# Second batch's attention: scores to ScalarE slot by slot, with the maximum as bias and the sum beside

## The chip, the cores and the metric

One core of a Trainium2 chip runs the whole program as one launch. The time is that of the device, in microseconds, as the median of the runs shown. The profile is of one more execution, which has a time of its own.

The engines of the core are named as the profile names them: PE is TensorE (PEld its weight loads), DVE is VectorE, ACT is ScalarE, POOL is GpSimd, SP issues most DMAs. Each engine takes its instructions strictly in the order in which the program wrote them, and waits for the other engines by semaphores.

## The reference

Three stages in a row, all in float32.

- Attention over 2 batches, 8 heads, 576 positions, head size 64. Heads 0 to 3 see the 32 latest positions (local); heads 4 to 7 see earlier positions with the same remainder modulo 32 (strided):

```python
scores = scale * q @ k.T                      # scale = 1/8
scores = where(mask, scores, -1e9)
scores = scores - max(scores, -1)
attn = exp(scores)
attn = attn / (sum(attn, -1) + 1e-9)
x = attn @ v                                  # then 1152 tokens x 512
```

- A gated product: `a = x @ w1; b = x @ w2; h = (a * b) @ w3; x = h @ w_out`.
- Four experts, mixed by given probabilities: `out += p_e * (relu(x @ w1_e) @ w2_e)`.

## The kernel before

Every large product is made of three matmuls on a high and a low part of both operands (`mm3`, L264 to L268, which is why L266, L267 and L268 carry nearly all the matmuls of the profile). ScalarE rounds to the high part, VectorE subtracts for the low one.

**Attention** is cut into chunks (`Chunk4`): per batch three local ones (c = 0, 1, 2 of g = 0) and three strided ones (g = 1), so six, numbered 0 to 5 below. A local chunk holds 6 slots of 64 score columns in one PSUM bank, a strided one 8 slots of 54. Each of the 128 partitions is one query row of its slot. A chunk goes through `scores` (PE), `maxima` (L367: VectorE takes the maximum of each slot and writes scores minus maximum to a frame `p_ring` in SBUF), `exps` (L380: one ScalarE activation over the whole frame, with the scale 1/8), `sums` (L383: VectorE sums each slot, adds 1e-9, takes the reciprocal), `normalise` (L394: VectorE in the second batch, GpSimd in the first), `transposes` (PE, into a PSUM bank), `evac` (L403: ScalarE copies it to SBUF), `pv` (PE, into two banks), `put` (ScalarE, high part of the result) and `put_lo` (VectorE, low part).

**Order.** All of it is in an order written out by hand (`tc.manual_schedule`, L748). The first batch's chunks run alone at the start (L816 to L848). The second batch's six chunks are woven into the first batch's gated product: `run_unit` (L772) emits one unit of that product, two accumulations of 12 matmuls each; ScalarE copies the first accumulation out (L503), VectorE multiplies it with the second (L505). After units 2, 4, 5, 7, 8, 10, 11, 13 and 14 comes one call of `attend` (L787). Call s emits, in this order: the scores of chunk s+1, `maxima` and `exps` of chunk s, `sums` and `normalise` of chunk s-1, `pv`, `put` and `put_lo` of chunk s-3, `transposes` and `evac` of chunk s-2. Below, "step s" is what follows the maximum of chunk s, until that of chunk s+1.

Each unit also calls a worker twice (`advance`, L256) which turns the next weights from 64-bit to 32-bit floats: ScalarE rounds (L143) and takes the magnitude (L151), VectorE clamps (L154), shifts (L157), adds the sign (L160) and the low bits (L164); then ScalarE makes the high part (L172) and VectorE the low one (L182). A unit can't start before the weights it uses are ready.

**Buffers.** Products, transposes and `pv` share five PSUM banks (`ps`); scores have three of their own (`ps_sc`). A bank that a transpose filled comes free when `evac` is through, one that a product filled when L503 or L505 is.

GpSimd in the second batch only does one small memset per strided chunk (L374, for the 1e-9 in the sum).

Of the kernel before, what the change touches and what calls it, by code (L numbers as in the profile page):

```python
# [8 lines left out]
F32 = mybir.dt.float32  # L9
# [4 lines left out]
AF = mybir.ActivationFunctionType  # L14
# [4 lines left out]
P = 128  # L19
# [13 lines left out]
SCALE = 1.0 / float(D) ** 0.5  # L33
# [9 lines left out]
def kernel(  # L43
# [13 lines left out]
    nc = tc.nc  # L57
# [8 lines left out]
    small = ctx.enter_context(tc.tile_pool(name="small", bufs=4))  # L66
# [254 lines left out]
    class Chunk4:  # L321
# [45 lines left out]
        def maxima(self):  # L367
            s = self.slots
            mx = small.tile([P, 8], F32, tag="mx", name="mx")
            nc.vector.tensor_reduce(out=mx[:, :s], in_=self.sc, axis=mybir.AxisListType.X, op=ALU.max)  # L370
            self.frame = p_ring[self.index % 4]
            self.p = self.frame[:, :s, :self.nk]
            if self.g:
                nc.gpsimd.memset(self.frame[:, :, T3:T3 + 1], 1e-9)  # L374
            nc.vector.tensor_tensor(out=self.p, in0=self.sc, in1=self.wide(mx), op=ALU.subtract)
# [2 lines left out]
            return t[:, :self.slots].unsqueeze(2).to_broadcast([P, self.slots, self.nk])  # L378

        def exps(self):  # L380
            nc.scalar.activation(self.p, self.p, AF.Exp, scale=SCALE)

        def sums(self):  # L383
            s = self.slots
            self.rec = small.tile([P, 8], F32, tag="rec", name="rec")
            rec = self.rec[:, :s]
            if self.g:
                nc.vector.tensor_reduce(out=rec, in_=self.frame[:, :s, :T3 + 1], axis=mybir.AxisListType.X, op=ALU.add)
            else:
                nc.vector.tensor_reduce(out=rec, in_=self.p, axis=mybir.AxisListType.X, op=ALU.add)  # L390
                nc.vector.tensor_scalar_add(rec, rec, 1e-9)
            nc.vector.reciprocal(rec, rec)
# [188 lines left out]
    class Weights:  # L581
# [17 lines left out]
        def work(self):  # L599
# [20 lines left out]
            if self.again:  # L620
                for i, u in enumerate(sums):
                    nc.sync.dma_start(out=u.bitcast(F32), in_=stored[self.at][i])
            else:
                yield from self.split(sums, w)
                for i, u in enumerate(sums):
                    nc.sync.dma_start(out=stored[self.at][i], in_=u.bitcast(F32))
# [394 lines left out]
```

## Time and profile before

| | |
|---|---|
| runs shown | 626.92, 626.93, 627.87 us; median 626.93 us |
| the profiled execution | 628.45 us, its span 626.3 us |
| PE busy | 615.6 us, 98% of the span |
| VectorE busy | 450.4 us, 72% |
| ScalarE busy | 265.0 us, 42% |
| GpSimd busy | 10.1 us, 2% |
| mean granted clock of PE | 0.997 of full |
| second batch's chunks, first maximum to last `put_lo` | 42.7 to 96.7 us |

A row of a timeline gives start, duration, engine, line, operation, what is written and read, and in brackets the idle time of that engine before it, with the instruction that ended it. Merged instructions carry their count (x2). Durations overlap at the ends: on ScalarE the next instruction starts about 0.1 us before the end of the one before it, if it has nothing to wait for. A busy PE is a PE with matmuls under way, not one at its peak.

### The profile page before, as it was taken

The numbers are of one execution on the slowest core, as the hardware profiler recorded it, in microseconds if no ns is written. First come the engines' busy times: TensorE is split into PE (matmuls) and PEld (weight loads), VectorE is DVE, ScalarE is ACT, GpSimd is POOL, SyncE is SP. The second block draws the span as 40 slices with busy tenths as digits, with TensorE's granted clock in tenths as the row PEclk, the third lists the DMA queues.
The fourth block names the chain that finished last, engine by engine and source line by source line (L and its number), as shares of the span: only waits on it lengthen the run. The fifth ranks groups of instructions, "written<-read, shape, count | busy, mean of one in ns | idle before, by whom it ended". The sixth has DMA issues, their size and how long they took to land.

```text
span 626.3 us, 11330 instructions
## 1 busy us (share of the span) xinstructions
PE 615.6 (98%) x4632; PEld 559.5 (89%) x4632; DVE 450.4 (72%) x813; ACT 265.0 (42%) x455; POOL 10.1 (2%) x37
## 2 busy tenths in 40 slices
PE   8899999999999999999999999999999999999997
PEld 5598899999889999999989999899889898989996
DVE  4889995989784224867977888788775665755843
ACT  3564574765654123433343433434433333333320
POOL 4100000000000000000000000000000000000000
PEclk9899999999999999999999999999999999999999
DMA  8876330235522210344344344354586566565411
GB/s 262 291 272 190 127 137 2 92 124 186 205 78 97 95 68 1 135 163 174 135 166 170 136 173 163 135 188 159 196 297 253 181 224 219 186 214 189 154 49 67
DMA packets 28726, 99.43 MB, mean 159 GB/s; under 512 B 2652, under 2 KB 6740, under 8 KB 26116
## 3 DMA queue, kind: packets, MB, share of 16 engines
q1 hardware_dynamic: 28132, 98.14, 44.5%
q8 instruction: 36, 0.59, 0.4%
q10 hardware_dynamic: 544, 0.59, 0.3%
q14 instruction: 14, 0.11, 0.1%
HBM read 79.58 MB, written 19.14 MB: 158 GB/s over the span
## 4 chain that ended last, share of the span: by engine, by line
PE 88%; DVE 4%; DMA 3%; ACT 3%; issue 2%; POOL 0%; SPq 0%; DVEq 0%
PE g_acc L266 11%; PE g_acc L267 11%; PE g_acc L268 10%; PE m_a L268 4%; PE m_a L267 4%; PE m_a L266 4%; PE m_b L267 3%; PE m_c L266 3%; PE x_acc L268 3%; PE x_acc L267 3%; PE x_acc L266 3%; PE m_c L267 3%; PE m_b L266 3%; PE m_c L268 3%; PE m_b L268 3%; PE ab_acc L266 3%
## 5 line engine op out<-in xcount | busy, mean ns | idle before, releaser
L657 ACT ACTIVATE h_hi<-u 128x320 fp32r<-128x320 f32 (+1 forms) x128 | 56.9, 445 | 189.0 <-DVE u L663 189.0
L266 PE MATMUL g_acc<-w_hi,h_hi 128*128 128x512 f32 (+1 forms) x296 | 114.3, 386 | 0.0
L267 PE MATMUL g_acc<-w_lo,h_hi 128*128 128x512 f32 (+1 forms) x296 | 114.2, 386 | 0.0
L268 PE MATMUL g_acc<-w_hi,h_lo 128*128 128x512 f32 (+1 forms) x296 | 113.7, 384 | 0.0
L596 DVE TENSOR_TENSOR w_lo<-raw,w_hi 128x768 fp32r<-128x768 f32 x64 | 69.4, 1084 | 12.4 <-ACT w_hi L594 12.4
L663 DVE TENSOR_TENSOR u<-m_b,u 128x320 f32<-128x320 f32 (+1 forms) x96 | 40.7, 452 | 51.1 <-PE m_b L268 51.1
L266 PE MATMUL ab_acc<-x_hi,w_hi 128*128 128x288 f32 x252 | 75.2, 298 | 1.3 <-ACT pT L406 1.0
L268 PE MATMUL ab_acc<-x_hi,w_lo 128*128 128x288 f32 x252 | 74.2, 294 | 0.0
L267 PE MATMUL ab_acc<-x_lo,w_hi 128*128 128x288 f32 x252 | 74.2, 294 | 0.0
L268 PEld LDWEIGHTS g_acc<-w_hi,h_lo 128*128 128x128 f32 x296 | 55.6, 188 | 11.6
L266 PEld LDWEIGHTS g_acc<-w_hi,h_hi 128*128 128x128 f32 x296 | 55.8, 188 | 8.0
L267 PEld LDWEIGHTS g_acc<-w_lo,h_hi 128*128 128x128 f32 x296 | 55.7, 188 | 7.6
L659 DVE SCALAR_TENSOR_TENSOR h_lo<-u,h_hi 128x320 fp32r<-128x320 f32 (+1 forms) x128 | 57.6, 450 | 3.6 <-ACT h_hi L657 1.8
L594 ACT CAST w_hi<-raw 128x768 fp32r<-128x768 f32 x64 | 59.9, 936 | 0.0
L266 PEld LDWEIGHTS ab_acc<-x_hi,w_hi 128*128 128x128 f32 x252 | 47.3, 188 | 2.0 <-ACT pT L406 1.2
L267 PEld LDWEIGHTS ab_acc<-x_lo,w_hi 128*128 128x128 f32 x252 | 47.3, 188 | 0.0
L268 PEld LDWEIGHTS ab_acc<-x_hi,w_lo 128*128 128x128 f32 x252 | 47.3, 188 | 0.0
L267 PE MATMUL m_b<-b_t,s_hi 128*128 128x320 f32 (+1 forms) x128 | 37.9, 296 | 0.0
L663 DVE TENSOR_TENSOR u<-m_a,u 128x320 f32<-128x320 f32 (+1 forms) x64 | 28.9, 451 | 11.6 <-PE m_a L268 11.6
L596 DVE TENSOR_TENSOR s_lo<-raw,s_hi 128x1024 fp32r<-128x1024 f32 x16 | 19.6, 1225 | 24.3 <-ACT s_hi L594 24.3
L663 DVE TENSOR_TENSOR u<-m_c,u 128x320 f32<-128x320 f32 (+1 forms) x64 | 29.0, 452 | 4.5 <-PE m_c L268 3.9
L673 ACT COPY u<-m_a 128x320 f32<-128x320 f32 (+1 forms) x32 | 12.7, 398 | 42.3 <-PE m_a L268 42.3
(162 smaller groups left out, 1398.2 us busy)
## 6 DMA issues: line engine op xcount, KB each, us to landing
raw<-in_e_dram SPq DMA_DIRECT2D x32, 1024.0 KB, 5.1
raw<-in_w_dram SPq DMA_DIRECT2D x8, 1024.0 KB, 6.4
raw<-in_w3T_dram SPq DMA_DIRECT2D x8, 1024.0 KB, 4.9
stored<-s_hi SPq DMA_DIRECT2D x16, 512.0 KB, 2.6
stored<-s_lo SPq DMA_DIRECT2D x16, 512.0 KB, 2.6
s_hi<-stored SPq DMA_DIRECT2D x16, 512.0 KB, 3.5
s_lo<-stored SPq DMA_DIRECT2D x16, 512.0 KB, 6.9
raw<-in_w_out_dram SPq DMA_DIRECT2D x4, 1024.0 KB, 8.4
```

What stands on the lines that cost most here:

```text
L266: mm(acc, lh, rh, start=first, stop=False)
L267: mm(acc, lh, rl, start=False, stop=False)
L268: mm(acc, ll, rh, start=False, stop=last)
L594: nc.scalar.copy(dst[0], src)
L596: nc.vector.tensor_tensor(out=dst[1], in0=src, in1=dst[0].bitcast(F32), op=ALU.subtract)
L657: nc.scalar.activation(hi, src, AF.Relu)
L659: nc.vector.scalar_tensor_tensor(out=lo, in0=src, scalar=0.0, in1=hi.bitcast(F32), op0=ALU.max, op1=ALU.subtract)
L663: nc.vector.tensor_tensor(out=out, in0=acc, in1=b, op=ALU.add)
L673: nc.scalar.copy(u1, a)
```

## The change

For the second batch (`self.b` is 1) alone:

- `maxima`: VectorE still takes the maximum of each slot. It no longer subtracts; GpSimd multiplies the maxima by -1/8 in place.
- `exps`: in place of one activation over the frame in SBUF, ScalarE runs one per slot (6 or 8). Each reads its scores from PSUM, takes the slot's scaled maximum as a bias column, and gives the slot's sum beside its result.
- `sums`: no summing on VectorE; GpSimd adds 1e-9 to the sums, VectorE takes the reciprocal as before.
- The memset of the 1e-9 column is gone for the second batch.

```diff
@@ maxima
             self.p = self.frame[:, :s, :self.nk]
+            if self.b:
+                self.mx = mx
+                nc.gpsimd.tensor_scalar_mul(mx[:, :s], mx[:, :s], -SCALE)
+                return
             if self.g:
                 nc.gpsimd.memset(self.frame[:, :, T3:T3 + 1], 1e-9)
             nc.vector.tensor_tensor(out=self.p, in0=self.sc, in1=self.wide(mx), op=ALU.subtract)
@@ exps
+            if self.b:
+                self.rec = small.tile([P, 8], F32, tag="rec", name="rec")
+                for s in range(self.slots):
+                    at = slice(s, s + 1)
+                    nc.scalar.activation(self.p[:, s], self.sc[:, s], AF.Exp, bias=self.mx[:, at], scale=SCALE,
+                                         accum_out=self.rec[:, at])
+                return
             nc.scalar.activation(self.p, self.p, AF.Exp, scale=SCALE)
@@ sums
             s = self.slots
-            self.rec = small.tile([P, 8], F32, tag="rec", name="rec")
+            if not self.b:
+                self.rec = small.tile([P, 8], F32, tag="rec", name="rec")
             rec = self.rec[:, :s]
-            if self.g:
+            if self.b:
+                nc.gpsimd.tensor_scalar_add(rec, rec, 1e-9)
+            elif self.g:
```

## Rows read from the trace of the kernel before

**Rows 1.** Waits of PE from 30 us on: total, times, longest.

```profile
PE ab_acc L266 <- ACT pT L406: 1.0, 1, 1.0
PE tp L401 <- DVE p_ring L396: 0.9, 1, 0.9
...
PE ab_acc L266 <- ACT ab L503: 0.3, 1, 0.3
```

**Rows 2.** Windows: stretch, length, busy time of each engine, PE clock, DMA, GB/s.

```profile
70.00:80.00 10.00, 9.02 (x109) 8.46 (x107) 9.79 (x18) 5.93 (x12) 0.00 (x0) 1.00 0.08 16
```

**Rows 3.** Timeline of VectorE, 42 to 78 us: start, duration, what.

```profile
42.73 0.55 DVE L370 TENSOR_REDUCE mx<-sc 128x6 f32<-128x384 f32 x1
...
44.75 0.46 DVE L505 TENSOR_TENSOR ab_f<-ab_acc,ab 128x288 f32<-128x288 f32 x1 [0.28 <-ACT ab L503]
...
50.20 0.55 DVE L370 TENSOR_REDUCE mx<-sc 128x6 f32<-128x384 f32 x1
...
53.71 1.21 DVE L182 TENSOR_TENSOR w_lo<-t,w_hi 128x1024 fp32r<-128x1024 f32 x1
...
55.45 0.55 DVE L370 TENSOR_REDUCE mx<-sc 128x6 f32<-128x384 f32 x1
...
60.62 0.68 DVE L154 TENSOR_SCALAR t<-t 128x1024 f32<-128x1024 f32 x1
...
63.56 0.60 DVE L370 TENSOR_REDUCE mx<-sc 128x8 f32<-128x432 f32 x1
...
66.21 0.61 DVE L458 TENSOR_TENSOR x_lo<-o,x_hi 128x192 fp32r<-128x192 f32 x2
...
69.37 0.60 DVE L370 TENSOR_REDUCE mx<-sc 128x8 f32<-128x432 f32 x1
...
71.93 0.61 DVE L458 TENSOR_TENSOR x_lo<-o,x_hi 128x192 fp32r<-128x192 f32 x2
...
77.92 0.60 DVE L370 TENSOR_REDUCE mx<-sc 128x8 f32<-128x432 f32 x1
```

**Rows 4.** Timeline of ScalarE, 43 to 81 us.

```profile
43.91 0.53 ACT L381 ACTIVATE p_ring<-p_ring 128x384 f32<-128x384 f32 x1 [3.25 <-DVE p_ring L375]
44.34 0.38 ACT L503 COPY ab<-ab_acc 128x288 f32<-128x288 f32 x1
44.62 1.05 ACT L172 CAST w_hi<-t 128x1024 fp32r<-128x1024 f32 x1
...
57.05 0.46 ACT L406 COPY pT<-tp 128x384 f32<-128x384 f32 x1
...
58.76 1.16 ACT L151 ACTIVATE t<-raw 128x1024 f32<-128x1024 f32 x1
...
79.67 0.52 ACT L454 CAST x_hi<-o 128x192 fp32r<-128x192 f32 x2
80.08 0.60 ACT L406 COPY pT<-tp 128x512 f32<-128x512 f32 x1
```

**Rows 5.** Timeline of PE: the `pv` of the second batch's chunk 3.

```profile
80.73 0.83 PE L427 MATMUL o<-pT,tv_str 54*64 54x54 f32 x32 [0.62 <-ACT pT L406]
```

**Rows 6.** Groups of ScalarE by shape: count, busy us, mean ns, idle before.

```profile
L381 ACT ACTIVATE p_ring<-p_ring 128x432 f32<-128x432 f32 x6 | 3.4, 566 | 12.7 <-DVE p_ring L375 12.7
...
L381 ACT ACTIVATE p_ring<-p_ring 128x384 f32<-128x384 f32 x6 | 3.1, 524 | 17.7 <-DVE p_ring L375 17.7
...
L111 ACT ACTIVATE one<-idle 128x1 f32<-128x1 f32 x1 | 0.2, 202 | 0.0
```

**Rows 7.** Timeline of all engines, 25.2 to 27 us, first batch's last chunk.

```profile
25.27 0.20 DVE L392 RECIPROCAL rec<-rec 128x8 f32<-128x8 f32 x1
...
25.61 0.92 POOL L396 TENSOR_TENSOR p_ring<-p_ring,rec 128x432 f32<-128x432 f32 x1 [2.90 <-DVE rec L392]
...
26.50 0.12 POOL L374 MEMSET p_ring<- 128x8 f32 x1
```

**Rows 8.** A window in the first batch, PE clock last but two.

```profile
17.00:23.00 6.00, 4.80 (x89) 3.64 (x85) 4.49 (x11) 2.94 (x8) 1.94 (x5) 0.72 0.85 320
```

## The prediction

> **What bounds the kernel now.** I read the waits of PE first. The page's first part has PE busy 98% of the span, so a change can only move the end by making PE wait more or less. From 30 us on PE waits for little: 1.0 us for ScalarE's copy of a transpose, 0.9 us for VectorE's normalised frame, 0.6 us for another such copy, 0.3 us later for L503 [rows 1, 5]. The first three lie in the second batch's attention, the stretch that the change touches. They are all that it could give back there: 0.6 + 0.9 + 1.0 = 2.5 us.
>
> Next the windows. In that stretch VectorE has hardly any idle time, 9.79 of 10 us from 70 to 80, ScalarE 5.93, GpSimd none [rows 2]. PE has run ahead and waits for the others. So VectorE's queue sets the pace there, and ScalarE stands idle 3.25 us in front of an exp until VectorE has subtracted [rows 4].
>
> Last the timelines of VectorE and ScalarE, to see what each does between one maximum and the next, and which of the two the other then waits for. The idle time of ScalarE is no free room: what stands behind the exp in its queue (the copies L503 and L406, the casts L454, the weights' L172 and L151) is what VectorE and PE wait for next.
>
> **What goes.** VectorE loses six subtractions, six sums and three additions of 1e-9, some 1.2 us a chunk, and gets a wait in their place: the reciprocal of chunk s-1 stands right behind the maximum of chunk s, and now needs GpSimd's addition, which stands in GpSimd's queue behind the multiplication for chunk s. POOL loses three memsets that nobody waited long for; I cost them at nothing. ScalarE loses six activations over a whole frame.
>
> **What comes, per slot.** 3 x 6 + 3 x 8 = 42 activations of 64 or 54 columns with a sum. No row shows one. Two bounds. From 384 to 432 columns an exp goes from 524 to 566 ns, 0.875 ns a column [rows 6]; carried down to 64 columns that is 524 - 320 x 0.875 = 244 ns. The next instruction on ScalarE starts 0.10 us before the end (43.91 + 0.53 to 44.34) [rows 4], so a bare one takes 0.145 us of the queue: the lower end, with bias column and sum for nothing. At the upper end the sum is an instruction of its own, as long as the shortest activation shown, 202 ns [rows 6], and nothing overlaps: 0.244 + 0.202 = 0.45 us. I take the sum as such an instruction that does overlap, 0.20 - 0.10 = 0.10, and for the bias column, which must be fetched too, 0.07 of the same 0.10: 0.145 + 0.10 + 0.07 = 0.32 us a slot. 1.92 us for a local chunk, 2.56 us for a strided one, where one activation took 0.43 us of the queue.
>
> The Trainium skill ("ScalarE: Activation LUTs", section "What ACT_TABLE_LOAD costs") prices an activation with a bias column at 280 ns plus 0.833 ns a column, less 93 ns overlap; without one at 186 ns. Its price without the column gives 506 ns for 384 columns, and the trace has 524, so they nearly agree. By it, with my 0.10 for the sum, a slot would cost 0.34 us (0.33 for 54 columns), and the sum below would be 7.5 us in place of 6.9. It speaks against this change: each slot pays the fixed part anew.
>
> **GpSimd.** From VectorE's end to a waiting GpSimd is 25.27 + 0.20 to 25.61, 0.14 us [rows 7]. Its multiplication of 6 or 8 columns lies between a memset of 8 columns, 0.12, and a product of 432, 0.92 [rows 7]; I take 0.20, near the memset. From there 0.04 us to ScalarE (as VectorE's maximum and subtraction to the exp). So the first slot starts 0.38 us behind the end of a maximum; the exp started 0.63 us behind it (42.73 + 0.55 to 43.91) [rows 3, 4].
>
> The Trainium skill ("SBUF — State Buffer", section "Who interferes with whom") says that a GpSimd instruction is held up while VectorE runs a one-input instruction in its two-port mode. Only chunk 0 has one there, the clamp that follows the maximum at once (later chunks have the waiting reciprocal). By that rule the first multiplication would start about 0.5 us later and the sum be 7.4 us; no row shows such a meeting, and I leave it out.
>
> **The sum, step by step.** Each step is measured from the end of a maximum to the first instruction that the later ScalarE holds up; the difference shifts all that follows on VectorE, the next maximum too. Slots end at 0.38 + 1.92 = 2.30 us behind the maximum in local chunks, at 0.38 + 2.56 = 2.94 in strided ones.
>
> - Step 0: the copy L503 stands behind the exp, 0.38 us long, and VectorE's product waits for it. After: 2.30 + 0.38 + 0.03 = 2.71. Before: 43.28 to 44.75, 1.47 [rows 3, 4]. Late by 1.24 us.
> - Step 1: L503, then 0.28 us later L172, 1.05 us long, and VectorE's L182 waits for it. After: 2.30 + 0.28 + 1.05 + 0.03 = 3.66. Before: 50.75 to 53.71, 2.96 [rows 3, 4]. Late by 0.70 us.
> - Step 2: `evac`, L503, L143 and the magnitude L151; from the first to the last 58.76 - 57.05 = 1.71, then 1.16. VectorE's clamp waits. After: 2.30 + 1.71 + 1.16 + 0.03 = 5.20. Before: 56.00 to 60.62, 4.62 [rows 3, 4]. Late by 0.58 us.
> - Step 3: the casts of `put` stand behind the exp; two start 0.205 us apart and end after 0.52, so the first takes 0.31 [rows 4]. `put_lo` waits for it. After: 2.94 + 0.31 + 0.04 = 3.29. Before: 64.16 to 66.21, 2.05 [rows 3]. Late by 1.24 us.
> - Step 4: the same. Before: 69.97 to 71.93, 1.96 [rows 3]. Late by 1.33 us.
> - Step 5: PE's `pv` of chunk 3 waits for `put` (0.41) and `evac` (0.60). After: 2.94 + 0.41 + 0.60 + 0.04 = 3.99. Before: 78.52 to 80.73, 2.21 [rows 3 to 5]. Late by 1.78 us.
>
> Sum: 1.24 + 0.70 + 0.58 + 1.24 + 1.33 + 1.78 = 6.87 us. PE waited for this very `pv` before, and afterwards waits for nothing but the 0.3 us of a later load [rows 1], so the lateness stays: no slack behind it takes it back. VectorE's saved work lies in front of these waits and turns into idle time there. PE's own waits at the transposes grow along the way but are no further term, since PE catches up only to the same copies.
>
> As a formula: 42 slots x their cost - 6.57 us. Zero at 0.156 us a slot; -0.5 us at the lower bound 0.145, +12.3 us at 0.45. GpSimd's share is six multiplications: a memset's 0.12 us each would take off 0.5 us, a product's 0.92 would add 4.3.
>
> Against the profiled execution's own 628.45 us this makes 635.3. That one stands 1.5 us above the median of the runs shown, 626.93; on the median the forecast is 633.8 us.
>
> **Rivals.**
>
> *PE's clock falls.* In six microseconds of the first batch in which PE was idle for 1.2 the granted clock was 0.72 on the mean, so part of them ran at the lower level, 1.2 GHz, and (1 - 0.72) x 6 = 1.7 us of PE were lost [rows 8]. In the changed kernel PE would wait about 0.62 + 1.78 = 2.4 us at `pv` of chunk 3, and as long in the two steps before. A drop in those is swallowed by the next wait; one behind the last isn't: 633.8 + 1.7 = 635.5. Against it: around these waits PE has dense products, which it hadn't in the first batch.
>
> *Slots at the upper bound.* Each sum is read only when its activation is through. For it: the sum does need the last column. +12.3 us, 639.3.
>
> *Slots as cheap as bare ones.* ScalarE then isn't late, and VectorE, 0.7 us a chunk better off, releases the frames and copies sooner; PE's three waits shrink. For it: VectorE is the engine without idle time [rows 2]. It decides below 0.156 us a slot. At 0.12 us the formula gives -1.5: 625.4; the waits of PE allow 624.4 at best. Against it: 0.12 is under the line through the exps.
>
> *It changes nothing that can be measured*: slots between 0.126 and 0.186, where gain and lateness cancel; 627.
>
> **How the numbers follow.** About 0.2% is what a measurement of this kernel can tell from no change, 1.25 us. Chances: forecast 0.65 (slots 0.20 to 0.43), clock 0.15, upper bound 0.10, no change 0.05, faster 0.05. So slower 0.90, same 0.05, faster 0.05. The range leaves out the last three, 0.20: low 629.0 is a slot of 0.20 (+1.8), high 638.5 one of 0.43 (+11.5) or a dearer slot than mine with a clock drop on top.
>
> **What would show it.** ScalarE has 42 short exps in six bursts, each 1.9 to 2.6 us; the time from one slot to the next is the number that decides. VectorE idles 1 to 2 us before L503's product in step 0 and before `put_lo` in steps 3 to 5, put down to ScalarE, and about 0.5 us before each reciprocal, put down to GpSimd. PE waits over 2 us three times for a copy of a transpose, and not later. After 95 us the two timelines run alike, some 7 us apart. The forecast is wrong if a slot costs under 0.19 us, if PE's waits don't grow, or if PE's clock row falls below 1.00 after 85 us.

## The result, and the profile after

The changed kernel takes 636.01 us, median of four runs (635.25 to 637.28); the kernel before, run beside it, 627.4. The ratio is 1.0135, 95% interval 1.0116 to 1.0154: slower, as forecast. The time is 2.2 us above the 633.8 of the prediction. The profiled execution took 635.94 us, with a span of 634.2 us against 626.3.

PE's waits from 30 us on in the changed kernel (what waited, for what; total us, times, longest), to be read against [rows 1]:

```profile
PE o L432 <- ACT pT L420: 2.4, 1, 2.4
PE o L441 <- ACT pT L420: 2.3, 1, 2.3
PE ab_acc L266 <- ACT ab L517: 1.2, 2, 0.8
PE tp L415 <- DVE p_ring L410: 1.0, 1, 1.0
PE ab_acc L266 <- DVE x_lo L472: 0.6, 1, 0.6
PE ab_acc L268 <- DVE w_lo L182: 0.4, 1, 0.4
PE ab_acc L512 <- ACT w_hi L172: 0.4, 1, 0.4
```

Two waits of over 2 us stand at `pv`, both for ScalarE's copy of a transpose (timeline of PE, chunks 1 and 3):

```profile
70.04 0.90 PE L432 MATMUL o<-pT,tv_loc 64*64 64x32 f32 x48 [2.40 <-ACT pT L420]
...
87.04 0.79 PE L441 MATMUL o<-pT,tv_str 54*64 54x54 f32 x32 [2.32 <-ACT pT L420]
```

The later one has grown from 0.62 [rows 5]; the earlier one is new, and the 1.0 at the product behind it has become 0.6. The wait for VectorE's normalised frame is what it was. VectorE's own part got shorter, and PE gained nothing from it.

ScalarE in the changed kernel, chunk 0 of the second batch (start, duration), to be read against the one exp in [rows 4]:

```profile
43.80 0.31 ACT L389 ACTIVATE p_ring<-sc,mx 128x64 f32<-128x64 f32 x1 [3.37 <-POOL mx L375]
44.01 0.19 ACT L389 ACTIVATION_READ_ACCUMULATOR p_ring<-sc,mx 128x1 f32 x1
44.10 0.30 ACT L389 ACTIVATE p_ring<-sc,mx 128x64 f32<-128x64 f32 x1
...
45.25 0.33 ACT L389 ACTIVATE p_ring<-sc,mx 128x64 f32<-128x64 f32 x1
45.45 0.23 ACT L389 ACTIVATION_READ_ACCUMULATOR p_ring<-sc,mx 128x1 f32 x1
45.54 0.42 ACT L517 COPY ab<-ab_acc 128x288 f32<-128x288 f32 x1
```

A slot is two instructions: an activation, and a readout of the accumulated sum that starts 0.20 us later; 0.09 us after that the next slot starts. From 43.80 to 45.54 are 1.74 us for six slots, 0.29 each. The copy L517, for which VectorE waits, stands behind all of them. The same instructions by shape (count, busy us, mean ns, idle before):

```profile
L389 ACT ACTIVATION_READ_ACCUMULATOR p_ring<-sc,mx 128x1 f32 x42 | 9.0, 213 | 0.0
L389 ACT ACTIVATE p_ring<-sc,mx 128x54 f32<-128x54 f32 x24 | 6.9, 316 | 6.4 <-POOL mx L375 6.4
L389 ACT ACTIVATE p_ring<-sc,mx 128x64 f32<-128x64 f32 x18 | 5.4, 318 | 9.0 <-POOL mx L375 9.0
```

Against [rows 6]: a slot of 54 columns is busy for 316 ns, a whole frame of 432 was for 566.

VectorE, in steps 0, 3 and 5 of the changed kernel, to be read against [rows 3]:

```profile
42.50 0.55 DVE L370 TENSOR_REDUCE mx<-sc 128x6 f32<-128x384 f32 x1
42.97 0.68 DVE L154 TENSOR_SCALAR t<-t 128x1024 f32<-128x1024 f32 x1
46.00 0.46 DVE L519 TENSOR_TENSOR ab_f<-ab_acc,ab 128x288 f32<-128x288 f32 x1 [2.35 <-ACT ab L517]
...
65.81 0.60 DVE L370 TENSOR_REDUCE mx<-sc 128x8 f32<-128x432 f32 x1
67.09 0.19 DVE L406 RECIPROCAL rec<-rec 128x6 f32<-128x6 f32 x1 [0.69 <-POOL rec L400]
...
69.42 0.62 DVE L472 TENSOR_TENSOR x_lo<-o,x_hi 128x192 fp32r<-128x192 f32 x2 [1.54 <-ACT x_hi L468]
...
86.31 0.62 DVE L472 TENSOR_TENSOR x_lo<-o,x_hi 128x192 fp32r<-128x192 f32 x2 [1.47 <-ACT x_hi L468]
```

In brackets is what became of the work that VectorE was spared: 2.35 us of waiting before the product of step 0, 0.7 to 0.8 before the reciprocals (all but the last), 1.4 to 1.5 before each `put_lo` of steps 3 to 5. From the end of the maximum to the held instruction step 0 now takes 46.00 - 43.05 = 2.95 us, where it took 1.47.

Last, windows of the changed kernel (stretch, length, busy time of PE, PEld, DVE, ACT, POOL; the granted clock is the last number but two), to be read against [rows 2]:

```profile
70.00:80.00 10.00, 9.38 (x99) 9.02 (x99) 7.42 (x14) 8.28 (x26) 0.51 (x2) 0.83 0.01 2
71.00:72.00 1.00, 1.00 (x8) 1.00 (x9) 1.00 (x3) 1.00 (x2) 0.00 (x0) 0.82 0.09 16
72.00:73.00 1.00, 1.00 (x6) 1.00 (x5) 1.00 (x2) 0.46 (x1) 0.00 (x0) 0.50 0.00 0
...
88.00:94.00 6.00, 6.00 (x36) 6.00 (x35) 5.50 (x11) 4.03 (x9) 0.00 (x0) 0.72 0.01 3
```

Between 70 and 80 us VectorE went from 9.79 us busy to 7.42 and ScalarE from 5.93 to 8.28: the pace has changed hands. (The two stretches don't hold quite the same work, since the changed kernel runs some 3 us behind there.) And PE's clock is at its lower level, 1.2 GHz (0.50), from about 71.6 to 75 us and again from about 88.7 to 92, each time 1.6 us after the end of one of the two long waits, with matmuls in between. The first fall loses (1 - 0.83) x 10 = 1.7 us of PE, the second (1 - 0.72) x 6 = 1.7. In the kernel before, the windows from 30 us on have the clock at 1.00.

### The profile page after: what moved, and what is told of

It reads as the page before. It is cut to its first block, busy times and chain, and to the rows that moved or that the text cites. A ratio compares the mean times of both kernels' runs of the same rounds, so it can differ in the third digit from the quotient of the medians.

```text
span 634.2 us, 11401 instructions
## 1 busy us (share of the span) xinstructions
PE 619.6 (98%) x4632; PEld 562.3 (89%) x4632; DVE 444.3 (70%) x798; ACT 274.6 (43%) x533; POOL 13.1 (2%) x46
## 4 chain that ended last, share of the span: by engine, by line
PE 83%; issue 5%; ACT 4%; DVE 3%; DMA 3%; POOL 0%; POOLq 0%; SPq 0%; DVEq 0%
PE g_acc L266 10%; PE g_acc L267 10%; PE g_acc L268 10%; PE m_a L268 4%; PE m_a L267 4%; PE m_a L266 4%; PE m_b L267 3%; PE m_c L266 3%; PE x_acc L268 3%; PE x_acc L267 3%; PE x_acc L266 3%; PE m_c L267 3%; PE m_b L266 3%; PE m_c L268 3%; PE m_b L268 3%
## 5 line engine op out<-in xcount | busy, mean ns | idle before, releaser
L266 PE MATMUL ab_acc<-x_hi,w_hi 128*128 128x288 f32 x252 | 76.7, 304 | 1.8 <-ACT ab L517 1.2
L268 PE MATMUL ab_acc<-x_hi,w_lo 128*128 128x288 f32 x252 | 75.7, 300 | 0.4 <-DVE w_lo L182 0.4
L267 PE MATMUL ab_acc<-x_lo,w_hi 128*128 128x288 f32 x252 | 75.7, 300 | 0.0
L266 PEld LDWEIGHTS ab_acc<-x_hi,w_hi 128*128 128x128 f32 x252 | 48.6, 193 | 2.7 <-ACT ab L517 1.7
L268 PEld LDWEIGHTS ab_acc<-x_hi,w_lo 128*128 128x128 f32 x252 | 48.7, 193 | 0.7 <-DVE w_lo L182 0.7
L267 PEld LDWEIGHTS ab_acc<-x_lo,w_hi 128*128 128x128 f32 x252 | 48.7, 193 | 0.0
```

The lines of the kernel that those rows point to most:

```text
L266: mm(acc, lh, rh, start=first, stop=False)
L267: mm(acc, lh, rl, start=False, stop=False)
L268: mm(acc, ll, rh, start=False, stop=last)
```

## The experiments

Theory A: the number of activations and readouts on ScalarE makes it late for the copies behind them in its queue, and PE's clock adds to it. The rivals put the cost on GpSimd's round trips, on the move of work as such, or on the clock alone. Ratios are against the kernel before, run beside each.

**e1: the small work on VectorE.** The multiplication and the addition leave GpSimd.

```diff
-                nc.gpsimd.tensor_scalar_mul(mx[:, :s], mx[:, :s], -SCALE)
+                nc.vector.tensor_scalar_mul(mx[:, :s], mx[:, :s], -SCALE)
-                nc.gpsimd.tensor_scalar_add(rec, rec, 1e-9)
+                nc.vector.tensor_scalar_add(rec, rec, 1e-9)
```

> The changed kernel, its small operations (times -1/8, plus 1e-9) on VectorE in place of GpSimd. Theory A (ScalarE's longer bursts make VectorE and PE late by some 6.3 us, and PE's clock falls once behind the last wait for 1.7 us): only the start of each burst moves. With GpSimd it starts 0.36 to 0.75 us behind a maximum; a small VectorE operation of 0.17 us and 0.03 us before it make that 0.24 us, so six times 0.13 and 0.4 in step 0: about 1.2 us less than the changed kernel, 634.8 us. Rival B (the two ways to GpSimd and back in each chunk are the cost: 0.38 us before the exps, 0.7 us before the reciprocal): some 6 us less, 630 or below.

632.87 us, ratio 1.0091 (1.0066 to 1.0115): between the two. PE's waits at `pv` were as long as before the edit, 2.3 and 2.1 us, so GpSimd didn't make them. But in the profiled execution the clock didn't fall behind them (its mean is 1.000):

```profile
70.00:76.00 6.00, 4.08 (x31) 3.85 (x30) 4.12 (x10) 4.97 (x22) 0.00 (x0) 1.00 0.00 0
88.00:94.00 6.00, 6.00 (x75) 5.78 (x74) 5.79 (x14) 4.16 (x6) 0.00 (x0) 1.00 0.10 15
```

So the 3 us under the changed kernel could be GpSimd's or the clock's; e17 takes that up.

**e2: the sums on VectorE.** No accumulating output; VectorE sums and adds as before the change, and GpSimd's memset of the 1e-9 column is back.

```diff
-                    nc.scalar.activation(self.p[:, s], self.sc[:, s], AF.Exp, bias=self.mx[:, at], scale=SCALE,
-                                         accum_out=self.rec[:, at])
+                    nc.scalar.activation(self.p[:, s], self.sc[:, s], AF.Exp, bias=self.mx[:, at], scale=SCALE)
...
-            if self.b:
-                nc.gpsimd.tensor_scalar_add(rec, rec, 1e-9)
-            elif self.g:
+            if self.g:
```

> The changed kernel without the sum beside the exp: VectorE sums each chunk again and adds the 1e-9 as in the kernel before; bias, slots and GpSimd's multiplication stay. The trace of the changed kernel has 0.095 us of ScalarE's queue for each reading of a sum. Theory A: 42 x 0.095 = 4.0 us less, since VectorE's sums fall into time in which it waited for ScalarE; 632.0 us, and 630.3 if PE's clock then doesn't fall. Rival B (GpSimd's round trips): one of two goes, about 3 us less, but then the time before each reciprocal shrinks and not the bursts. Rival D (VectorE's relief was worth something and is given back): slower than A says by the six sums, 3.4 us, so 635.5.

630.3 us, ratio 1.0051 (1.0035 to 1.0068): A, at its value for a clock that holds, though in the profiled execution the clock fell once, from 83 to 86 us. The timeline of its ScalarE, a local chunk and a strided one (the bare slots are merged, x6 and x8):

```profile
42.81 1.34 ACT L390 ACTIVATE p_ring<-sc,mx 128x64 f32<-128x64 f32 x6 [3.35 <-POOL mx L377]
44.01 0.43 ACT L515 COPY ab<-ab_acc 128x288 f32<-128x288 f32 x1
...
70.25 1.68 ACT L390 ACTIVATE p_ring<-sc,mx 128x54 f32<-128x54 f32 x8 [1.16 <-POOL p_ring L375]
71.77 0.59 ACT L466 CAST x_hi<-o 128x192 fp32r<-128x192 f32 x2
```

To the next instruction are 1.20 and 1.52 us: 0.20 and 0.19 a slot. The readout is the other 0.09. Six readouts less are 0.5 us a chunk that stood ahead of a held copy.

**e3: the split alone.** The kernel before, its exp cut into slots in SBUF; no bias column, no sum, VectorE and GpSimd untouched.

```diff
+            if self.b:
+                for s in range(self.slots):
+                    nc.scalar.activation(self.p[:, s], self.p[:, s], AF.Exp, scale=SCALE)
+                return
             nc.scalar.activation(self.p, self.p, AF.Exp, scale=SCALE)
```

> The kernel before with one edit: the second batch's exp of a frame is split into one activation per slot (42 in place of 6), from SBUF, without bias column and without sum; VectorE and GpSimd as before. A (the number of activations on ScalarE makes ScalarE late): a slot without the sum took 0.19 to 0.20 us of ScalarE's queue in the changed kernel; in the formula 42 x 0.195 - 6.57 = 1.6, plus the exp's start 0.63 in place of 0.38 us behind the maximum, 6 x 0.25 = 1.5: 3.1 at most, less where VectorE's own subtractions and sums still stand in front of the held instruction; 627.3 + 1 to 3.1 = 628.3 to 630.4. F (splitting alone costs nothing, the sums and GpSimd's part cost it all): 627.3 +- 0.5.

629.44 us, ratio 1.0030 (1.0017 to 1.0042): A, in the middle of its range. Its ScalarE:

```profile
43.54 1.00 ACT L383 ACTIVATE p_ring<-p_ring 128x64 f32<-128x64 f32 x6 [3.25 <-DVE p_ring L375]
44.44 0.38 ACT L507 COPY ab<-ab_acc 128x288 f32<-128x288 f32 x1
...
64.95 1.22 ACT L383 ACTIVATE p_ring<-p_ring 128x54 f32<-128x54 f32 x8 [3.05 <-DVE p_ring L375]
66.08 0.51 ACT L458 CAST x_hi<-o 128x192 fp32r<-128x192 f32 x2
```

0.90 us for six and 1.13 for eight: 0.15 and 0.14 us for a bare slot, the lower bound of the prediction. Even so 2 us are lost.

**e6: the changed kernel, with the exps out of the way.** They are issued behind the step's copies and casts and behind the next unit's first copy.

```diff
@@ attend
-                chunk[s].exps()
...
+            if s < n:
+                later.append(chunk[s].exps)
@@ run_unit, behind the first half of the next unit
+                for exps in later:
+                    exps()
+                later.clear()
```

> The changed kernel with each burst of exps emitted later in ScalarE's queue: behind put, evac and the next unit's first copy, with nothing else changed. Theory A: what VectorE and PE waited for now stands ahead of the burst, steps 0 and 3 to 5 lose their lateness, steps 1 and 2 (weights' casts behind the burst) keep some; PE no longer waits over 2 us, its clock stays up. Near the kernel before, 627 to 629 us. Rival B (GpSimd's round trips, which stay, all of them): no better than the changed kernel less 2 us, 634 or more.

626.5 us, ratio 0.9994 (0.9982 to 1.0006): A, half a microsecond under its range. Every instruction of the change is still there; only what stands behind the slots is another.

**e7: the same move in the kernel before.** It settles whether e6 undid a lateness or gained something else that hid it.

```diff
-                chunk[s].exps()
+            if s < n:
+                later.append(chunk[s].exps)
```

> The kernel before with one edit: the second batch's exp of a frame is issued on ScalarE behind the copies of the step and the next unit's first copy, as in e6, with one activation per frame and all of VectorE's work as before. A (in e6 the move only took the slots out of the way of the held instructions; the exp of before was 0.43 us of the queue, so the move has little to give): 626.3 to 627.3. G (the move itself gains several us, and the changed instructions cost as much in e6 as in the changed kernel, hidden by that gain): below 624, since e6 was 9.5 us faster than the changed kernel.

627.0 us, ratio 0.9991 (0.9975 to 1.0006): A. Over all executions the move alone is worth nothing that can be measured, and 1.3 us where the mean clock is 0.999 or more (medians 625.7 for six executions, 627.0 for 14 of the kernel before); in the changed kernel it was worth 9.5 us (636.0 to 626.5). So the place of the slots in ScalarE's queue is the cause, the clock included, as far as the queue brings it about.

**e10: the clock held up.** The changed kernel, with eight idle matmuls of 448 columns ahead of `pv` in steps 4 and 6.

```diff
                 c = chunk[s - 3]
+                if s in (4, 6):
+                    acc = ps_sc.tile([P, 512], F32, tag="sc", name="warm")
+                    for _ in range(8):
+                        mm(acc[:, :448], flat(i_loc), flat(m_loc), start=True, stop=True)
                 c.pv()
```

> The changed kernel with eight idle matmuls of 448 columns on PE ahead of pv in steps 4 and 6, that is inside the two waits of 2.3 to 2.4 us, into a bank of the scores. Theory A: the clock no longer falls behind either; the first fall was swallowed by the next wait, the second is worth 1.7 us, so 634.3 us; VectorE's and ScalarE's times up to pv of chunk 3 stay. Rival C (the clock is most of the loss, PE's waits would be hidden without it): 630 or below. Rival E (the clock costs nothing, it is the same lateness counted twice): 636, unchanged.

632.5 us, ratio 1.0080 (1.0053 to 1.0106), and the same two windows now read:

```profile
70.00:76.00 6.00, 5.65 (x82) 4.66 (x79) 4.28 (x8) 4.78 (x19) 0.51 (x2) 1.00 0.04 12
...
88.00:94.00 6.00, 6.00 (x52) 5.96 (x47) 5.60 (x12) 4.74 (x10) 0.00 (x0) 1.00 0.01 3
```

PE does more work and the kernel is 3.5 us faster by the medians. The idle matmuls also shorten the idle stretches: PE stands for 1.60 us ahead of the first eight, which wait for the exps to free a bank of scores, and for 0.78 us ahead of the later `pv`. The time is under the 634.3 that A expected, with the first fall swallowed by the next wait and the second worth 1.7; why, is said with the prediction below.

**e17: e1 with e10's idle matmuls.** Both edits are shown above.

> e1 (the two small instructions on VectorE) with the idle matmuls of e10 ahead of pv in steps 4 and 6, so that PE's clock is the same in both. K (with the clock held, it is all the same whether GpSimd or VectorE does the small work: e1 was 3.1 us under the changed kernel because the clock cost it less): as e10, 631.5 to 633.2, ratio 1.007 to 1.009. L (GpSimd's way there and back costs the 3 us itself): 629 to 630.3, ratio 1.003 to 1.005.

632.81 us, ratio 1.0087 (1.0063 to 1.0112), beside e10's 1.0080: K by the medians, and L's 3 us are excluded. A smaller price shows in the traces. From the start of the first maximum to `pv` of chunk 3 are 43.4 us in e1 and in e17, 44.6 in e10 and 44.5 in the changed kernel: GpSimd's way costs some 1.2 us up to there, as A had it in e1, and the medians don't resolve it. That e1 itself was no slower (1.0091), though its three other executions had a mean clock of 0.995, says that falls cost it little; why they did, and why its clock held in the profiled one, behind waits as long as those of the changed kernel, stays open.

**e18: e2 with idle matmuls.** Here they came to stand behind `pv` and `put`, not ahead of them as in e10, which the expectation did not reckon with.

> e2 (no accumulating output, sums on VectorE) with the idle matmuls of e10. A (42 readouts of 0.09 us of ScalarE's queue are the dearest part, with the clock held too): e10 less 3.8 us, 628.0 to 629.3, ratio 1.001 to 1.003. M (the readouts cost little, and e2 was faster because its clock fell once and not twice): 630.5 to 632.5, ratio 1.005 or more.

632.34 us, ratio 1.0077 (1.0056 to 1.0098). It does not decide between A and M: behind `pv` the 16 idle matmuls are on PE's path, and in one window the clock fell all the same:

```profile
82.00:88.00 6.00, 5.15 (x50) 3.57 (x51) 5.44 (x12) 3.46 (x10) 0.00 (x0) 0.72 0.18 74
```

The wait, 1.93 us, comes first, and the work after it didn't keep the clock up here. What the sums cost at full clock is seen otherwise: the executions of e2 with a mean clock of 0.999 or more took 629.6, 630.0 and 630.25 us, those of e10 632.1, 632.3 and 632.7. The sums on ScalarE, with GpSimd's addition, are worth some 2.3 us at the end; A had said 3.8. Up to `pv` of chunk 3 the traces are nearer to A: from the start of the first maximum 41.0 us in e2, 44.6 in e10.

**e13: what is good in the change.** e6 with e2's sums: the subtraction stays gone, the slots stand out of the way, and the reciprocal waits for nothing on GpSimd.

> The changed kernel with two edits: exps behind the copies as in e6, and the sums back on VectorE (no accumulating output; the sum and the addition of 1e-9 as the kernel before has them), so that the reciprocal waits for nothing on GpSimd; the slots still read PSUM with the scaled maximum as bias, and VectorE has no subtraction. A (what stays of the change is then VectorE's saved subtractions, and the slots are out of the way): the six waits of 0.69 to 0.82 us for GpSimd in e6 go, six sums of about 0.4 us come back: 626.5 - 6 x (0.75 - 0.4) = 624.4, range 623.5 to 626. H (GpSimd's round trip costs nothing in e6, VectorE only waits there instead of later): 626.5 + up to 2.4 = 627 to 629.

Its edits are those of e2 and e6. 624.23 us, ratio 0.9946 (0.9927 to 0.9965): A; faster than both kernels. PE's waits from 30 us on are down to:

```profile
PE tp L413 <- DVE p_ring L408: 0.9, 1, 0.9
PE ab_acc L510 <- ACT w_hi L172: 0.4, 1, 0.4
```

The median is 2.8 us under e7's, but half of e7's executions have a mean clock of 0.997 (626.9 to 629.0 us; in the profiled one it falls behind a wait of 1.70 us). With 0.999 or more, e7 has a median of 625.7 and e13 of 624.2: the six subtractions that VectorE is spared are worth about 1.5 us, if nothing else waits for the slots.

**e8: another way to the same place.** e7 with the second batch's normalising product on GpSimd, one activation per frame.

```diff
-            engine = nc.vector if self.b else nc.gpsimd
+            engine = nc.gpsimd
```

> The kernel before with two edits: exps behind the copies as in e7 (one activation per frame), and the second batch's normalising product of a frame on GpSimd, as the first batch has it (0.92 us there). A (VectorE has no idle time in this stretch, so work taken off it moves the end up to what PE's waits allow, 2.5 us): 627.3 - 2 to 2.5 = 624.8 to 625.3. I (GpSimd's product is later than VectorE's and the transposes wait for it): 627.3 to 630.

624.25 us, ratio 0.9947 (0.9928 to 0.9966): faster, as A and a little more. VectorE set the pace of the kernel before, and the 0.5 us a chunk taken off it shows, since ScalarE isn't made late. Three of the six products on GpSimd (timeline of GpSimd):

```profile
51.01 1.08 POOL L396 TENSOR_TENSOR p_ring<-p_ring,rec 128x384 f32<-128x384 f32 x1 [25.54 <-DVE rec L392]
55.89 1.62 POOL L396 TENSOR_TENSOR p_ring<-p_ring,rec 128x384 f32<-128x384 f32 x1 [3.80 <-DVE rec L392]
...
63.74 0.83 POOL L396 TENSOR_TENSOR p_ring<-p_ring,rec 128x384 f32<-128x384 f32 x1 [6.17 <-DVE rec L392]
```

One and the same product takes 0.83 to 1.62 us; what holds it up there was not tried.

**e14 and e16: further along.** e14 is e13 with e8's edit; e16 is e13 with the first pair of lines of e1.

> e13 with one more edit: the second batch's normalising product of a frame on GpSimd, as in e8. A (VectorE still sets the pace in e13, where PE waits 0.9 us for its normalised frame and 0.4 us for a weight): at most those 0.9 us less than e13, 623.3 to 624.2. I (GpSimd's product, 0.92 us in the first batch, is later than VectorE's and takes the room that the saved work gives, as in e8, where PE waits 1.4 us for it): 624.2 to 625.

> e13 with the multiplication by -scale on VectorE in place of GpSimd, so that VectorE has one small instruction more a chunk, right behind the maximum. A (in e13 the slots stand behind the copies, so nothing waits early for the multiplication, and VectorE pays for six small instructions, 0.1 to 0.2 us each, where it sets the pace): 624.2 + 0 to 1.2 = 624.2 to 625.4. J (GpSimd's multiplication, 0.62 us beside VectorE's clamp in chunk 0 and then 0.36 to 0.44 us behind the maximum, still makes the slots late in e13): under 624.0.

625.13 us, ratio 0.9955 (0.9935 to 0.9975), and 624.44 us, ratio 0.9927 (0.9903 to 0.9951). e14 brings no more than e13: in its profile PE waits 1.6 us for GpSimd's product, as theory I has it. (That execution took 630.01 us, 4.9 above the median; PE also waits 2.6 us for a copy at 147.70.) e16 can't be told from e13 either, which is A and not J. e8, e13 and e16 can't be told apart: 3 to 5 us faster than the kernel before, by their ratios.

## Why the prediction was right, and where not

Right: the direction, the mechanism, and the range. The time came out as that of the clock rival (635.5), to which I gave 0.15, and not as that of the likeliest case. I had put down as a sign against the forecast that PE's clock falls below 1.00 after 85 us, and it does. That 633.8 came within 2.2 us is in part luck: the slots were costed 1.5 us too dear, and the clock's 1.7 us at nothing.

*The slot.* Its three terms were 0.145 + 0.07 + 0.10 = 0.32 us. Measured: 0.145 for a bare one (e3), 0.05 more for the bias column and the source in PSUM, which no run tells apart (e2 less e3), 0.09 for the readout (changed kernel less e2): 0.285. That the sum is an instruction of its own which overlaps, about as long as the shortest one shown (202 ns; it is 213), was right. The term was 0.035 us a slot too high, 1.5 us in all. By the formula: 42 x 0.285 - 6.57 = 5.4.

The Trainium skill ("ScalarE: Activation LUTs", section "What ACT_TABLE_LOAD costs") has the duration nearly right, 280 + 0.833 x 64 = 333 ns against the row's 318. By its overlap of 93 ns a slot without a sum would take 0.24 us of the queue (an estimate); the rows of e2 show 0.20.

*GpSimd.* The first slot was to start 0.38 us behind the end of a maximum. From the second chunk on it is 0.36 to 0.44. In chunk 0 it is 43.80 - 43.05 = 0.75, because the multiplication took 0.62 us there and not 0.24 (timeline of GpSimd in the changed kernel):

```profile
43.14 0.62 POOL L375 TENSOR_SCALAR mx<-mx 128x6 f32<-128x6 f32 x1 [16.90 <-DVE mx L370]
52.08 0.24 POOL L375 TENSOR_SCALAR mx<-mx 128x6 f32<-128x6 f32 x1 [8.32 <-DVE mx L370]
...
66.49 0.25 POOL L375 TENSOR_SCALAR mx<-mx 128x8 f32<-128x8 f32 x1 [8.04 <-DVE mx L370]
```

It ends at 43.76, 0.1 us behind VectorE's clamp (42.97 + 0.68 = 43.65). That is the meeting which I left out; it adds 0.4 us. e2, e6, e10, e13 and e18 have the same row, 0.61 to 0.63 us, each ending 0.1 us behind the clamp. The rule of the Trainium skill that I weighed ("SBUF — State Buffer", section "Who interferes with whom"), by which GpSimd is held up until a one-input instruction of VectorE in its two-port mode is through, agrees with these rows; in which mode the clamp ran, no row shows. The multiplication of chunk 0 is also the first after 16.9 us without work, and no run tells that from the meeting.

*The six steps.* Late by, forecast and measured: step 0, 1.24 and 1.48; step 1, 0.70 and 0.55; step 2, 0.58 and 0.41; step 3, 1.24 and 0.96; step 4, 1.33 and 1.13; step 5, 1.78 and 1.59; together 6.87 and 6.12. Five are smaller by the cheaper slots, step 0 is larger by GpSimd. One place I had not seen: behind step 4 VectorE's L182 waits 0.27 us for L172. From the start of the first maximum to `pv` of chunk 3 were 80.73 - 42.73 = 38.0 us and are now 87.04 - 42.50 = 44.5: 6.5 us, nearly all of them in these steps.

*The sum without the clock.* 5.4 + 0.4 = 5.8 us. The profiled execution of e10, where the clock holds in the second batch, took 633.87 us, 5.4 above the 628.45 of the kernel before; in both the clock falls once in the first batch. So the working of the forecast stands, with its two terms corrected. Against the profiled execution the forecast was 635.3, and 635.94 came. On the medians the gap is wider because I took off 1.5 us, by which the median of the kernel before lay under its profiled execution; that of the changed kernel, 636.01, doesn't lie under its own.

*The step that failed* is the one on the clock: "around these waits PE has dense products", as a reason against a fall. Dense products follow the waits, but the clock falls in spite of them, twice in the profile. The other half, "A drop in those is swallowed by the next wait", came true. In e10 the clock doesn't fall at 71 us, and these are its first maximum and its `pv` of chunk 3:

```profile
42.70 0.55 DVE L370 TENSOR_REDUCE mx<-sc 128x6 f32<-128x384 f32 x1
...
87.33 0.79 PE L441 MATMUL o<-pT,tv_str 54*64 54x54 f32 x32 [0.78 <-ACT pT L420]
```

That is 44.6 us, where the changed kernel has 44.5 with the fall. The slower PE only ate part of its own next wait (0.58 us, 1.33 in e10). The second fall is not swallowed. From that `pv` to the end of the span are 547.2 us in the changed kernel and 544.8 in e10: 2.4 us, of which 1.7 are the fall and 0.8 the later wait below, which e10 doesn't have. So the rival had the price right, and I gave it too small a chance. The two profiled executions, 635.94 and 633.87 us, are 2.1 apart. The medians are 3.5 apart, and there the clocks differ by more: three of e10's four executions have a mean clock of 0.999 or 1.000, so hardly a fall in the first batch either, those of the changed kernel 0.992 to 0.995.

*No slack behind it*: right. After 88 us PE waits once, for L517 at 154.87 (0.78 us, one of the two in that row; 0.31 before [rows 1]). Nothing is taken back; 0.5 us is added, at a load that I had counted as unchanged. That wait differs between profiled executions, from none in e10 to 1.23 us in e1.

## What to carry to other kernels

An instruction that is cheap by its columns is dear by its count: cutting six activations into 42 cost more of ScalarE's queue than the spared work gave VectorE, and where it ended up was decided by what stands behind it in that queue. So before moving work to an idle engine, read what the engine does next and who waits for that; here the same 42 activations behind the copies, with the sums left where they were, turned 8.5 us of loss into 3 us of gain. A wait of PE of about 2 us can cost more than its length, since the clock may fall after it (1.7 us here, where no later wait took it up).

## What the runs showed of the hardware

- An accumulated sum on ScalarE is an instruction of its own: 213 ns busy on the mean of 42, 0.09 us of the queue.
- A bare exp of 54 or 64 columns takes 0.14 to 0.15 us of ScalarE's queue from SBUF; with a bias column and from PSUM 0.19 to 0.20.
- A GpSimd multiplication of 6 columns took 0.24 us, and 0.62 us while VectorE ran a clamp of 1024 columns (the first work of GpSimd after 16.9 us, too).
- PE's clock went to 1.2 GHz after waits of 2.40 and 2.32 us (changed kernel), 1.91 (e2), 1.93 (e18) and 1.70 (e7), with matmuls under way again, and lost 1.7 us each time. It did not fall after waits up to 1.0 us in the kernel before from 30 us on, nor after 1.72 in e6, nor in one execution (e1) after 2.28, 1.92 and 2.14. Idle matmuls ahead of the waiting instruction, which also cut the idle stretches to 1.6 and 0.8 us, kept it at 2.4 GHz; such matmuls behind it did not.
- A fall with a wait for other engines behind it cost nothing up to that wait's end: 44.5 us from the first maximum to `pv` of chunk 3 with a fall at 71 us, 44.6 without (e10).
